# A state-space block and a SiLU layer on one core: the last second product with tokens on the partitions, and one transpose moved between engines

## The chip, the core and the metric

The kernel runs on one core of a Trainium2 chip. The metric is the device time of one execution in microseconds (us); lower is better. Before the change the median of three runs is 352.27 us (352.03 to 353.18). Five engines matter: TensorE (PE for its matmuls, PEld for its weight loads), VectorE (DVE), ScalarE (ACT), GpSimd (POOL) and SyncE (SP, which here only issues transfers).

## The reference

Two blocks follow each other. The first is a chunked scan (batch 4, 8 heads, 768 tokens, head width 32, state width 16), the second a two-layer network with SiLU on its result, seen as 3072 tokens of 256 features.

```python
# first block, per batch and head, in chunks of tokens
L = np.exp(cum[:, :, :, None] - cum[:, :, None, :]) * causal
M = np.einsum('bhin,bhjn->bhij', Cc, Bc) * L
y = np.einsum('bhij,bhjd->bhid', M, xc) + np.einsum('bhin,bhnd->bhid', Cc, state) * decay_to_i[..., None]
state = decay_full[..., None, None] * state + np.sum(Bx, axis=2)   # Bx: B times x, with the decay to the chunk's end
# second block: x is y as (3072, 256); w_in (256, 2048), w_out (2048, 256)
h = x @ w_in
g = h * (1.0 / (1.0 + np.exp(-h)))
out = g @ w_out
```

## The kernel before

The 3072 tokens are cut into 12 units of 256. For each unit the kernel does the scan with small tiled matmuls and then the network. Units go through the network in pairs. From the fourth unit on, the first product (`h = x @ w_in`), and for all pairs the second (`g @ w_out`), are done with seven block products instead of eight (a Strassen-Winograd form): some operands are first added or subtracted, and the seven results are added up afterwards. All data is fp32; every fp32 matmul call shows in the trace as two records.

The first unit's data comes in as follows. `load_n` loads B as tokens x (head, n), and `load_t` loads in a layout from which a 32x32 block transpose on VectorE (`f_T`) gives (head, n) x tokens. C of unit 0 comes by `load_t`, B of unit 0 by `load_n` alone, and TensorE transposes it (`f_TP`):

```python
load_t(0, 1, nc.sync)          # C of unit 0, four transfers
load_n(0, 0, nc.scalar)        # B of unit 0, tokens on the partitions, two transfers
nc.sync.dma_start(out=pa01, in_=...)   # the decays of units 0 and 1, one row per (head, n)
load_x(0, nc.sync)
for n in range(3):
    load_w(n, nc.sync)         # weights of 512 KB a piece, as raw bits
...
def f_T(u, i):                 # i = 0: B, i = 1: C
    t = (BH, CT)[i][u] = sc.tile([128, UT], FP32, name=("bh", "ct")[i])
    nc.vector.transpose(out=..., in_=tbc[u][:, i]...)

def f_TP(u):
    tp = ps_o.tile([128, 512], FP32, name="o_ps")
    for i, t in enumerate((bn[u],) if u == 0 else (bn[u], tbc.pop(u))):
        for k in range(2):
            nc.tensor.transpose(out=tp[:, 256 * i + 128 * k:...], in_=t[:, k]..., identity=ident)
    BH[u] = sc.tile([128, UT], FP32, name="bh")
    nc.scalar.activation(BH[u], tp[:, 0:256], AF.Copy)
    if u == 1:
        CT[u] = sc.tile([128, UT], FP32, name="ct")
        nc.scalar.activation(CT[u], tp[:, 256:512], AF.Copy)
    elif u > 1:
        CT[u] = tp[:, 256:512]          # stays in PSUM
def f_T2(u, e): ...   # ScalarE: ce = CT with the heads of one parity, needed by the product f_G0
def f_C(u): ...       # cw = CT * decays, on VectorE for u == 2, else on GpSimd
```

The order at the start (one queue per engine, in this order):

```python
f_T(0, 1)                       # VectorE: ct
for e in range(2): f_T2(0, e)   # ScalarE: ce
f_Ab(0, 0); f_Ab(0, 1)          # TensorE: decays to a PSUM tile
f_TP(0)                         # TensorE and ScalarE: bh
busy(0, 18)                     # TensorE: 18 small bf16 matmuls, fillers[...]
f_G0(0); busy(4, 8)             # TensorE: bh x ce, and fillers
f_Ek(0, 0); f_Ek(0, 1)          # VectorE: scans into E
f_B(0)                          # GpSimd: BT = bn * E
f_D0(0, True)                   # TensorE: BT x x
f_P01()                         # VectorE: pa01, clipped and scanned
f_C(0); f_S(0); f_SM(0)         # GpSimd: cw; VectorE: the states st; ScalarE
for k in range(2): f_M(0, k)    # VectorE: E = E * product
w_size(0); w_bits(0, 2)         # ScalarE, VectorE, GpSimd: piece 0 of the weights rebuilt from raw bits
...
f_Ek(1, 1); f_B(1); f_C(1); w_bits(2, 2); f_D0(1, True); f_G0(1); f_S(1)
...
```

The second product of a pair holds the weights still (`lhsT`) and moves 256 tokens of g, so the results have output features on the partitions. `f_out` transposes them in 32x32 blocks on VectorE and stores them in runs of 128 bytes, four transfers each. For the last pair (`final`) it is the same, but for the last product, which TensorE transposes in two halves:

```python
for n, (m, w, g) in enumerate(segs):        # products 1, w, 5, 7, 6, 4, 3
    o = ...                                 # a PSUM tile of 128 x 256
    for j in range(NF // 2):                # 8
        nc.tensor.matmul(out=o, lhsT=w(j), rhs=g()[:, j], start=(j == 0), stop=(j == last))
        if j == last:
            end(m, o)
        yield
# in end(m, o), for the last product of the last pair:
elif m == "3" and final:
    for k in range(2):
        nc.vector.tensor_tensor(out=pn[:, :, k], in0=on[:, :, k], in1=p["6"]..., op=ALU.add)
        tp = ps_h.tile([128, 512], FP32, name="hp")[:, 0:128]
        nc.tensor.transpose(out=tp, in_=p["3"][:, 128 * k:128 * k + 128], identity=ident)
        ot = opool.tile([128, UT], FP32, name="ot")[:, 0:128]
        if k == 0: nc.scalar.activation(ot, tp, AF.Copy)
        else:      nc.vector.tensor_copy(out=ot, in_=tp)
        (nc.sync, nc.scalar)[k].dma_start(out=out[r:r + 128, 0:128], in_=ot)
```

Of the kernel before, what the change touches and what calls it, by code (L numbers as in the profile page):

```python
# [8 lines left out]
FP32 = mybir.dt.float32  # L9
U32 = mybir.dt.uint32  # L10
BF16 = mybir.dt.bfloat16
AF = mybir.ActivationFunctionType
ALU = mybir.AluOpType
# [8 lines left out]
def kernel(  # L22
# [22 lines left out]
    nc = tc.nc  # L45

    batch, H, S, D = x.shape
    N = B.shape[-1]
    Q = 64
    UT = 256  # L50
    UPB = S // UT
    NU = batch * UPB
    d_model, d_ff = moe_w_in.shape
    NF = d_ff // 128
# [8 lines left out]
    sc = ctx.enter_context(tc.tile_pool(name="sc", bufs=1))  # L63
# [4 lines left out]
    ppool = ctx.enter_context(tc.tile_pool(name="ppool", bufs=5))  # L68
    opool = ctx.enter_context(tc.tile_pool(name="opool", bufs=2))
    ps_s = ctx.enter_context(tc.tile_pool(name="ps_s", bufs=1, space=bass.MemoryType.PSUM))  # L70
    ps_h = ctx.enter_context(tc.tile_pool(name="ps_h", bufs=3, space=bass.MemoryType.PSUM))
# [5 lines left out]
    pa, ab, bn, tbc, xt = ({} for _ in range(5))  # L77

    def at(u):
        return u // UPB, u % UPB * UT  # L80
# [28 lines left out]
    def load_t(u, i, q):  # L109

        b, t0 = at(u)
        if u not in tbc:
            tbc[u] = loads.tile([128, 2, 2, 8, N], FP32, name="tbc")
        for g in range(4):
            q.dma_start(out=tbc[u][32 * g:32 * g + 32, i],
                        in_=(B, C)[i][b, 2 * g:2 * g + 2, t0:t0 + UT].rearrange("e (t r) n -> t e r n", r=8))
# [76 lines left out]
    QZ = 8 * (Q + 1)  # L193
    pa01 = flat[:, 6 * UT:8 * UT]
    pz01, one01, pfx01 = (flat[:, 8 * UT + QZ * i:8 * UT + QZ * (i + 1)] for i in range(3))
    load_t(0, 1, nc.sync)
    load_n(0, 0, nc.scalar)
    nc.sync.dma_start(out=pa01, in_=bass.AP(tensor=a.tensor, offset=a.offset, ap=[[S, H], [0, N], [1, 2 * UT]]))
# [22 lines left out]
    def busy(n, small=0):  # L221
        t = ps_o.tile([128, 512], FP32, name="o_ps")
        for i in range(n):
            nc.tensor.matmul(out=t, lhsT=idle[:, 0:128], rhs=idle, start=True, stop=True)
        for i in range(small):
            nc.tensor.matmul(out=t[:64, :64], lhsT=idle[:, 0:64], rhs=idle[:, 64:128], start=True, stop=True)
# [20 lines left out]
    ident = const.tile([128, 128], FP32, name="ident")  # L247
# [22 lines left out]
    E, M, BT, BH, CT, CE, CW, PFX, ST, SM, DP, XM, GTS, BX = ({} for _ in range(14))  # L270
# [65 lines left out]
    def f_B(u, engine=nc.gpsimd):  # L336

        BT[u] = sc.tile([128, 2, H, N], FP32, name="BT")
        engine.tensor_tensor(out=BT[u], in0=bn[u], in1=E[u][:, :, :, Q - 1:Q].to_broadcast([128, 2, H, N]),  # L339
                                op=ALU.mult)  # L340

    def f_T(u, i):

        t = (BH, CT)[i][u] = sc.tile([128, UT], FP32, name=("bh", "ct")[i])
        nc.vector.transpose(out=t.rearrange("p (t r) -> p r t", r=8), in_=tbc[u][:, i].rearrange("p e r n -> p r e n"))
        if i == 1:
            tbc.pop(u)

    def f_TP(u):

        tp = ps_o.tile([128, 512], FP32, name="o_ps")
        for i, t in enumerate((bn[u],) if u == 0 else (bn[u], tbc.pop(u))):
            for k in range(2):
                nc.tensor.transpose(out=tp[:, 256 * i + 128 * k:256 * i + 128 * k + 128],
                                    in_=t[:, k].rearrange("p h n -> p (h n)"), identity=ident)
        BH[u] = sc.tile([128, UT], FP32, name="bh")
        nc.scalar.activation(BH[u], tp[:, 0:256], AF.Copy)
        if u == 1:

            CT[u] = sc.tile([128, UT], FP32, name="ct")  # L360
            nc.scalar.activation(CT[u], tp[:, 256:512], AF.Copy)
        elif u > 1:
            CT[u] = tp[:, 256:512]

    def f_T2(u, e):

# [4 lines left out]
    def f_C(u):  # L371

        CW[u] = sc.tile([128, UT], FP32, name="cw")
        engine = nc.vector if u == 2 else nc.gpsimd
        engine.tensor_tensor(out=CW[u].rearrange("p (c t) -> p c t", t=Q),
                             in0=CT.pop(u).rearrange("p (c t) -> p c t", t=Q), in1=PFX[u][:, :, 1:], op=ALU.mult)

# [131 lines left out]
    SO, TN, PEND = {}, {}, []  # L509
# [44 lines left out]
    def f_out(P, i, v, c):  # L554
# [4 lines left out]
        for q in range(4):  # L559
# [2 lines left out]
                            ap=[[d_model, 32], [32 * d_model, UT // 32], [1, 32]]),  # L562
                in_=t[32 * q:32 * q + 32].rearrange("p (b d) -> p b d", d=32))

    def s2_pair(P, final=False, joint=False):

        adder = nc.vector if final else nc.gpsimd
        p = {}
        segs = (("1", lambda j: wjo[:, 0, 0, j], lambda: gb(P, 0, 0)), ("w", lambda j: wjo[:, 1, 0, j], lambda: gb(P, 1, 0)),
                ("5", lambda j: SO[0][j // 4][:, j % 4], lambda: TN[P]),  # L570
                ("7", lambda j: SO[2][j // 4][:, j % 4], lambda: gb(P, 0, 1)),
                ("6", lambda j: SO[1][j // 4][:, j % 4], lambda: gb(P, 0, 0)),
                ("4", lambda j: wjo[:, 1, 1, j], lambda: gb(P, 1, 0)),
                ("3", lambda j: SO[3][j // 4][:, j % 4], lambda: gb(P, 1, 1)))

        def end(m, o):

            p[m] = ppool.tile([128, UT], FP32, name="ps")
            on = o.rearrange("p (c k t) -> p c k t", c=2, k=2)
            pn = p[m].rearrange("p (k c t) -> p c k t", c=2, k=2)  # L580
            if not (final and m == "3"):
                nc.scalar.activation(pn, on, AF.Copy)  # L582
            if m == "w":
                p_add(p["w"], p["w"], p["1"], adder)
                PEND.append(partial(f_out, P, 0, 0, p["w"]))
            elif m == "6":
                p_add(p["6"], p["6"], p["1"], adder)
                p_add(p["7"], p["7"], p["6"], adder)
                p_add(p["6"], p["5"], p["6"], adder, ALU.subtract)
                p_add(p["5"], p["5"], p["7"], adder, ALU.subtract)  # L590
                PEND.append(partial(f_out, P, 1, 1, p["5"]))
            elif m == "4":
                p_add(p["4"], p["4"], p["7"], adder)
                PEND.append(partial(f_out, P, 1, 0, p["4"]))
            elif m == "3" and final:

                for k in range(2):
                    nc.vector.tensor_tensor(out=pn[:, :, k], in0=on[:, :, k],
                                            in1=p["6"].rearrange("p (k c t) -> p c k t", c=2, k=2)[:, :, k],
                                            op=ALU.add)  # L600

                    tp = ps_h.tile([128, 512], FP32, name="hp")[:, 0:128]
                    nc.tensor.transpose(out=tp, in_=p["3"][:, 128 * k:128 * k + 128], identity=ident)
                    ot = opool.tile([128, UT], FP32, name="ot")[:, 0:128]
                    if k == 0:
                        nc.scalar.activation(ot, tp, AF.Copy)
                    else:
                        nc.vector.tensor_copy(out=ot, in_=tp)
                    b, t0 = at(2 * P + 1)
                    r = b * S + t0 + 128 * k  # L610
                    (nc.sync, nc.scalar)[k].dma_start(out=out[r:r + 128, 0:128], in_=ot)
            elif m == "3":
                p_add(p["3"], p["3"], p["6"], adder)
                PEND.append(partial(f_out, P, 0, 1, p["3"]))

        last = NF // 2 - 1
        if joint:
            o = ps_o.tile([128, 2, UT], FP32, name="o_ps")
            for j in range(NF // 2):
                for n, (m, w, g) in enumerate(segs[:2]):  # L620
                    nc.tensor.matmul(out=o[:, n], lhsT=w(j), rhs=g()[:, j], start=(j == 0 and n == 0), stop=(j == last),  # L621
                                     skip_group_check=True)
                    if j == last and n == 1:
                        end("1", o[:, 0])
                        end("w", o[:, 1])
                    yield
        for n, (m, w, g) in enumerate(segs):
            if joint and n < 2:
                continue
            if final and n % 2 == 0:  # L630
                o = ps_h.tile([128, 2, UT], FP32, name="hp")[:, 0]
            else:
                o = ps_o.tile([128, 2, UT], FP32, name="o_ps")[:, 0]
            for j in range(NF // 2):
                nc.tensor.matmul(out=o, lhsT=w(j), rhs=g()[:, j], start=(j == 0), stop=(j == last))  # L635
                if j == last:
                    end(m, o)
                yield
# [157 lines left out]
        return plan  # L796


    f_T(0, 1)
    for e in range(2):  # L800
        f_T2(0, e)
    f_Ab(0, 0)
    f_Ab(0, 1)
    f_TP(0)
    busy(0, 18)
    f_G0(0)
    busy(4, 8)
    f_Ek(0, 0)
# [25 lines left out]
    f_s1(0, 1)  # L834
    f_Ek(1, 1)
    f_B(1)
    f_C(1)
    w_bits(2, 2)
    f_D0(1, True)
    f_G0(1)  # L840
    f_S(1)
# [152 lines left out]
```

## Time and profile before

The profile is that of one execution of 350.6 us from the first to the last instruction. In four stretches, from the answer by windows:

| stretch, us | what runs | PE busy, us | DVE busy, us | ACT busy, us | POOL busy, us | DMA share |
|---|---|---|---|---|---|---|
| 0 to 25.19 | units 0 and 1 of the scan, first weights | 21.65 | 21.91 | 13.67 | 11.77 | 0.79 |
| 25.19 to 321.41 | network of all pairs, other scans | 296.22 | 170.08 | 146.20 | 98.82 | 0.64 |
| 321.41 to 345.59 | second product of the last pair | 24.18 | 12.72 | 2.87 | 2.94 | 0.15 |
| 345.59 to 350.57 | the end | 0.75 | 0.78 | 0.28 | 0.00 | 0.17 |

A busy figure is the time in which an engine had an instruction in work; small fillers on TensorE count as busy too. TensorE's records overlap, as its matmuls are pipelined: a record lasts longer than the distance to the next one. In the chain of work that ended last, each line gives a start, a duration and what ran there; the duration reaches to the next link, so it can be shorter than the instruction. In a timeline, "x16" after a group is the number of records merged into the line, and the bracket at its end is the idle time of the engine before it and what ended it.

### The profile page before, as it was taken

How to read it: one execution, taken by the hardware profiler on the slowest of the kernel's cores; microseconds unless marked ns; L12 is line 12 of the kernel's file. 1: busy time of each engine (PE TensorE's matmuls, PEld its weight loads, DVE VectorE, ACT ScalarE, POOL GpSimd, SP SyncE). 2: the span in 40 equal slices, each digit the busy share in tenths (PEclk: the TensorE clock that was granted, in tenths of full speed). 3: DMA queues.
4: the chain of work that ended last, by engine and by line, in shares of the span. 5: the costliest groups of instructions: out<-in, count | busy, mean ns of one | idle time of the engine just before them, and what ended most of it. 6: DMA issues, size and time to landing. Idle time of an engine off the chain costs nothing.

```text
span 350.6 us, 8353 instructions
## 1 busy us (share of the span) xinstructions
PE 342.8 (98%) x3308; PEld 287.7 (82%) x3308; DVE 205.5 (59%) x406; ACT 163.0 (46%) x398; POOL 113.5 (32%) x141
## 2 busy tenths in 40 slices
PE   7989999999999999999999999999999999999995
PEld 3668888888888888888888888888888888888883
DVE  7998889976795665543763553664562322244821
ACT  3677674323323545455544454645445454553100
POOL 4455335444285122244042244042144112051200
PEclk9999999999999999999999999999999999999999
DMA  6977987799776788964189964067404337521202
GB/s 129 214 247 174 263 270 137 133 202 212 133 128 116 129 169 157 175 129 76 24 165 171 163 121 83 16 118 140 78 2 75 65 57 136 90 54 30 36 4 46
DMA packets 117056, 42.66 MB, mean 122 GB/s; under 512 B 102424, under 2 KB 108824, under 8 KB 117016
## 3 DMA queue, kind: packets, MB, share of 16 engines
q1 hardware_dynamic: 110328, 25.67, 35.4%
q0 software_dynamic: 4464, 16.25, 24.6%
q8 instruction: 26, 0.43, 0.5%
q10 hardware_dynamic: 2224, 0.20, 0.5%
q14 instruction: 14, 0.11, 0.1%
HBM read 22.70 MB, written 3.15 MB: 74 GB/s over the span
## 4 chain that ended last, share of the span: by engine, by line
PE 91%; DVE 4%; issue 1%; DMA 1%; POOL 0%; ACT 0%; SPq 0%; DVEq 0%; ACTq 0%
PE o_ps L635 36%; PE hp L690 28%; PE hp L499 15%; PE hp L635 3%; PE gy L471 2%; PE o_ps L621 2%; PE gy L408 2%; PE gy L462 2%; DVE wv L178 1%; PE gy L393 1%; DVE E L419 1%; DVE E L302 1%; DMA gT<-in_a_dram 1%; DVE st L434 0%; DVE wu L174 0%
## 5 line engine op out<-in xcount | busy, mean ns | idle before, releaser
L693 DVE TENSOR_TENSOR gT<-hp,p 128x256 f32<-128x256 f32 x64 | 26.9, 420 | 73.9 <-ACT p L704 37.9
L499 PE MATMUL hp<-XM,w_in_sb 128*128 128x256 f32 x256 | 59.5, 382 | 1.6 <-POOL w_in_sb L182 1.4
L635 PE MATMUL o_ps<-gT,w_out_sb 128*128 128x256 f32 x240 | 60.4, 380 | 0.0
L696 ACT ACTIVATE gT<-gT 128x256 f32<-128x256 f32 x96 | 39.7, 414 | 44.0 <-DVE gT L693 44.0
L499 PEld LDWEIGHTS hp<-XM,w_in_sb 128*128 128x128 f32 x256 | 47.8, 190 | 9.8 <-POOL w_in_sb L182 2.9
L690 PE MATMUL hp<-raw 128*128 128x256 f32 x192 | 52.7, 380 | 0.0
L552 POOL TENSOR_TENSOR ps<-ps 128x256 f32<-128x256 f32 x35 | 29.4, 839 | 70.8 <-ACT ps L582 68.9
L635 PEld LDWEIGHTS o_ps<-gT,w_out_sb 128*128 128x128 f32 x240 | 45.5, 190 | 6.3
L547 POOL DMA_DIRECT2D gT<-gT x31 | 27.2, 914 | 67.8 <-DVE TN L538 21.5
L690 PEld LDWEIGHTS hp<-raw 128*128 128x128 f32 x192 | 36.2, 190 | 5.3 <-POOL ps L552 0.6
L704 ACT ACTIVATE p<-hp 128x256 f32<-128x256 f32 x64 | 24.5, 383 | 27.4 <-PE hp L690 26.0
L693 DVE TENSOR_TENSOR gT<-hp,u 128x256 f32<-128x256 f32 x32 | 13.6, 424 | 38.8 <-PE hp L690 38.8
L690 PE MATMUL hp<-XM,w_in_sb 128*128 128x256 f32 x128 | 34.1, 389 | 0.0
L501 ACT ACTIVATE gT<-hp 128x512 f32<-128x512 f32 x32 | 19.0, 594 | 26.9 <-PE hp L499 26.8
L690 PEld LDWEIGHTS hp<-XM,w_in_sb 128*128 128x128 f32 x128 | 23.3, 190 | 4.2 <-issue 0.9
L582 ACT ACTIVATE ps<-o_ps 128x256 f32<-128x256 f32 x38 | 14.4, 382 | 23.9 <-PE o_ps L635 19.8
L302 DVE TENSOR_TENSOR_SCAN E<-ab,diag 128x256 f32<-128x256 f32 (+1 forms) x32 | 25.3, 831 | 0.4
L339 POOL TENSOR_TENSOR BT<-bn,E 128x256 f32<-128x256 f32 x12 | 9.9, 824 | 46.5 <-DVE E L302 37.7
L635 PE MATMUL o_ps<-gT,wu 128*128 128x256 f32 x88 | 22.4, 380 | 0.0
L635 PE MATMUL o_ps<-gT,wv 128*128 128x256 f32 x88 | 22.2, 380 | 0.0
L635 PE MATMUL o_ps<-gT,raw 128*128 128x256 f32 x80 | 20.5, 380 | 0.0
L690 PE MATMUL hp<-raw,w_in_sb 128*128 128x256 f32 x64 | 19.1, 380 | 0.0
(125 smaller groups left out, 522.1 us busy)
## 6 DMA issues: line engine op xcount, KB each, us to landing
gT<-gT POOLq DMA_DIRECT2D x31, 512.0 KB, 6.1
ab<-in_a_dram SPq DMA_DIRECT2D x40, 128.0 KB
raw<-in_moe_w_in_dram SPq DMA_DIRECT2D x8, 512.0 KB
raw<-in_moe_w_out_dram SPq DMA_DIRECT2D x8, 512.0 KB
xt<-in_x_dram SPq DMA_DIRECT2D x24, 128.0 KB
out_dram<-ot SPq DMA_DIRECT2D x92, 32.0 KB
bn<-in_B_dram SPq DMA_DIRECT2D x22, 64.0 KB
tbc<-in_C_dram SPq DMA_DIRECT2D x40, 32.0 KB
```

Source lines behind the costliest of these rows:

```text
L302: nc.vector.tensor_tensor_scan(out=E[u].rearrange("p k h t -> p (k h t)")[:, Q * g0:Q * (g0 + n)], data0=t.rearrange("p g t -> p (g t)"), ...
L339: engine.tensor_tensor(out=BT[u], in0=bn[u], in1=E[u][:, :, :, Q - 1:Q].to_broadcast([128, 2, H, N]), op=ALU.mult)
L499: nc.tensor.matmul(out=hp[:, i], lhsT=w_in_sb[:, kc, f * 128:(f + 1) * 128], rhs=xm[:, kc], start=(kc == 0), stop=(kc == KC - 1))
L501: nc.scalar.activation(GTS[g][:, :, j], hp, AF.Silu)
L547: nc.gpsimd.dma_start(out=o[:, js], in_=a[:, js], accum_op=ALU.add)
L552: engine.tensor_tensor(out=o, in0=p, in1=q, op=op)
L582: nc.scalar.activation(pn, on, AF.Copy)
L635: nc.tensor.matmul(out=o, lhsT=w(j), rhs=g()[:, j], start=(j == 0), stop=(j == last))
L690: nc.tensor.matmul(out=o, lhsT=w, rhs=x_, start=start, stop=True, skip_group_check=True)
L693: nc.vector.tensor_tensor(out=o, in0=p, in1=q, op=ALU.add)
L696: nc.scalar.activation(o, i, AF.Silu)
L704: nc.scalar.activation(o, i, AF.Copy)
```

## The change

It has three parts. The second product of the last pair, all seven block products, is turned round: g is held still and the weights move, in two halves of 128 tokens, so results have tokens on the partitions and go out as rows of 512 bytes, without any transposes; the last product is added and stored by halves. B of unit 0 is loaded a second time in the layout for VectorE, with four transfers on ScalarE's queue, and transposed there in place of TensorE. And C of unit 1 stays in PSUM, with its product with the decays on VectorE in place of GpSimd, behind piece 2 of the weights.

```diff
+    load_t(0, 0, nc.scalar)
     load_t(0, 1, nc.sync)
     load_n(0, 0, nc.scalar)
...
     def f_TP(u):
-        for i, t in enumerate((bn[u],) if u == 0 else (bn[u], tbc.pop(u))):
+        for i, t in enumerate((bn[u], tbc.pop(u))):
...
         nc.scalar.activation(BH[u], tp[:, 0:256], AF.Copy)
-        if u == 1:
-            CT[u] = sc.tile([128, UT], FP32, name="ct")
-            nc.scalar.activation(CT[u], tp[:, 256:512], AF.Copy)
-        elif u > 1:
-            CT[u] = tp[:, 256:512]
+        CT[u] = tp[:, 256:512]
...
-        engine = nc.vector if u == 2 else nc.gpsimd
+        engine = nc.vector if 0 < u < UPB else nc.gpsimd      # UPB is 3
...
+    def f_rows(P, i, v, t):
+        for c in range(2):
+            f_row(P, i, v, t, c, (nc.sync, nc.scalar)[c])
+    def f_row(P, i, v, t, c, q):
+        b, t0 = at(2 * P + v)
+        q.dma_start(out=bass.AP(tensor=out.tensor, offset=out.offset + (b * S + t0 + 64 * c) * d_model + 128 * i,
+                                ap=[[128 * d_model, 2], [d_model, 64], [1, 128]]),
+                    in_=t[:, 128 * c:128 * c + 128])
...  # in end(): f_rows in place of f_out for the last pair, and for its product "3" no transposes
-            elif m == "3" and final:
-                ...
...
+            if final:
+                if m == "3":
+                    p[m] = ppool.tile([128, UT], FP32, name="ps")
+                for c in range(2):
+                    ts = slice(128 * c, 128 * c + 128)
+                    for j in range(NF // 2):
+                        nc.tensor.matmul(out=o[:, ts], lhsT=g()[:, j, ts], rhs=w(j), start=(j == 0), stop=(j == last))
+                        if j == last and m == "3":
+                            nc.vector.tensor_tensor(out=p[m][:, ts], in0=o[:, ts], in1=p["6"][:, ts], op=ALU.add)
+                            f_row(P, 0, 1, p[m], c, nc.sync)
+                        elif j == last and c == 1:
+                            end(m, o)
+                        if j % 2:
+                            yield
+                continue
...
-    f_T(0, 1)
+    for i in range(2):
+        f_T(0, i)
...
-    f_TP(0)
-    busy(0, 18)
+    busy(0, 20)
...
-    f_C(1)
-    w_bits(2, 2)
+    w_bits(2, 2)
+    f_C(1)
```

## The prediction

> **What bounds the kernel now.** I read the busy line of the page first, then the chain of work that ended last in order of time, then the timelines of the first 26 and the last 10 us, and last the groups by form for single durations.
>
> ```profile
> PE 342.8 (98%) x3308; PEld 287.7 (82%) x3308; DVE 205.5 (59%) x406; ACT 163.0 (46%) x398; POOL 113.5 (32%) x141
> ```
>
> TensorE is busy for 98% of the span, so only three things can move the end: how soon its unbroken stream begins, how long the stream is, and what follows its last matmul. The chain of the first stretch:
>
> ```profile
> 4.87 0.66 DVE ct L345
> 5.53 0.02 issue
> 5.55 0.91 ACT ce L369 x2
> 6.46 0.28 ACT bh L357
> 6.73 0.04 issue
> 6.78 0.73 PE o_ps L226 x18
> ...
> 9.46 0.42 PE hp L393 x32
> 9.89 0.02 issue
> 9.91 0.23 DVE st L432
> ...
> 24.41 0.74 POOL w_in_sb L182
> 25.15 0.04 issue
> 25.19 12.36 PE hp L499 x56
> ```
>
> The columns are start, duration, and what ran. Until 9.9 us the work passes from VectorE to ScalarE to TensorE, from there to 24.3 us it is VectorE almost throughout, and at 25.19 us TensorE gets the weights that it waited for. The waits of TensorE after that come to nothing, up to its last matmul at 345.4 us. So a change of the early path moves the end by the same amount. The tail:
>
> ```profile
> 342.13 3.62 PE L635 MATMUL hp<-gT,raw 128*128 128x256 f32 x16
> ```
> ```profile
> 345.79 0.49 DVE L598 TENSOR_TENSOR ps<-hp,ps 128x128 f32<-128x128 f32 x2 [2.09 <-PE hp L635]
> ...
> 346.13 0.59 PE L603 MATMUL hp<-ident,ps 128*128 128x128 f32 x2 [0.39 <-DVE ps L598]
> 346.50 0.28 ACT L606 ACTIVATE ot<-hp 128x128 f32<-128x128 f32 x1 [3.73 <-PE hp L603]
> 346.80 0.36 SPq L611 DMA_DIRECT2D out_dram<-ot  x1
> 346.90 0.29 DVE L608 COPY ot<-hp 128x128 f32<-128x128 f32 x1 [0.62 <-PE hp L603]
> 347.22 0.37 ACTq L611 DMA_DIRECT2D out_dram<-ot  x1
> ```
>
> After the last product come two additions, two transposes by TensorE, two copies and two stores; the second store is issued at 347.22 us, 1.43 us after the first addition began, and the span ends at 350.57.
>
> **What the Trainium skill says.** (1) "TensorE: Matmul & The Clock Gate", section "Back-to-back issue gap": a warm matmul of N columns follows the one before after N/2.4 + 2.5 ns, but a stream of weight load and matmul pairs ran at 81 ns for N = 128, where the formula gives 56. The trace: 16 records of 256 fp32 columns took 3.62 us, (3.62 - 0.38)/15 = 0.216 us each, so fp32 takes two array cycles a column, with only a few ns on top. It has no 128x128 product of 128 columns, so which of the two figures holds is the open question here. (2) The same page, "LDWEIGHTS (loading the stationary operand)": the load time follows the columns of the stationary operand, not its rows. The groups by form agree: fp32 loads of 32, 64 and 128 columns last 105, 131 and 190 ns. (3) "SBUF - State Buffer", section "Who interferes with whom": a VectorE instruction with two SBUF inputs contends with a GpSimd instruction that reads SBUF. The trace agrees: the merge of weight bits (L178) takes 0.68 us alone, and 1.22 and 1.17 us at 14.88 and 19.36 us, when GpSimd works. (4) "DMA: Bandwidth & Descriptors", section "Anatomy of one DMA": about 2 us of a DMA are fixed, most of it the receipt of the write. By the trace's semaphore records the store issued at 346.81 had landed at 348.36, the one of 347.22 at 348.81 but for one engine at 349.42: 1.55 to 2.2 us.
>
> **Part 1: the second product of the last pair.** Its seven products are 56 calls of two records each, 112 records of 256 moving columns: 321.41 to 345.59 us, 24.18 us. Afterwards each is two halves of 128 tokens, so 224 records of 128 moving columns and as many weight loads of 128 columns. The columns streamed are the same; each load now has to hide behind half the streaming, 108 ns (half of 216). What may be tight is the load. Its 190 ns are mostly latency: the transposes load 128 columns in 140 ns and still follow each other every 0.11 us, and bf16 fillers with loads of 112 ns every 31 ns:
>
> ```profile
> 6.78 0.73 PE L226 MATMUL o_ps<-gT 128*64 128x64 bf16 x18 [0.58 <-ACT bh L357]
> ...
> 37.39 0.38 PE L354 MATMUL o_ps<-ident,bn 128*128 128x128 f32 x2
> 37.61 0.38 PE L354 MATMUL o_ps<-ident,tbc 128*128 128x128 f32 x2
> ```
>
> The fillers: (0.73 - 0.20)/17 = 31 ns, with 64 columns loaded and 64 streamed, some 27 ns at one cycle a column, so equal load and stream overlap with 4 ns lost. The streaming part of an fp32 load of 128 columns, from the growth of the durations: (190 - 105)/96 = 0.89 ns a column, 113 ns; from the transposes,[...] 190 - 140 = 50 ns a pass, 100 ns. So I take a pitch of 109 to 115 ns, 111 in the middle: 224 x 0.111 = 24.9 us, **+0.7 us** (+0.2 to +1.6). All of it is on the path. The VectorE transposes that go away (0.45 us each) and the stores as rows lie beside the matmuls and give nothing here.
>
> **Part 2: the tail.** The last half's product ends, VectorE adds 128 columns (0.29 us, after the same 0.2 us from the last streamed column), and SyncE stores. The last column streams at 345.59; addition at 345.79 to 346.08, store at about 346.11 instead of 347.22: 1.1 us earlier. The first half went out some 16 records (1.8 us) before. If this store lands in 1.55 us and no engine is late, a further 0.6 us goes. From landing to end stays 350.57 - 349.42 = 1.15 us. Together **-1.1 to -1.7 us**, -1.4 in the middle.
>
> **Part 3: the start.** Removed: two transposes and the 0.36 us copy of bh on ScalarE, which stands in the chain at 6.46. Added: a second block transpose on VectorE; the pitch of one to the scan after it is 5.36 - 4.87 = 0.49 us, and it stands before the transpose that feeds ce. So ce is done at 6.46 + 0.49 = 6.95, and the first product can start there, 0.5 us before the old 7.43; but VectorE's own row (two scans, 2.27 us, and the P pair, 2.03 us) now begins at 5.85 and ends at 10.16, where st could start at 9.91: **+0.25 us**. Four more loads also stand ahead of the other loads. There are eight completion semaphores in turn, so the load of pa01, issued at 3.07 us, must wait until an earlier load has landed (the C loads landed at 3.5 to 4.5 us): some 0.5 us later. It landed at 7.63 us, just when VectorE wanted it (7.65); half a us later it would land at about 8.1 to 8.6, against 8.14 wanted: +0 to +0.4 us more. For unit 1, the decay product cw leaves GpSimd for VectorE (0.40 us, as the PSUM form at 42.44 us), behind the bits of piece 2; with GpSimd quiet the merge at 19.36 us should take 0.68 instead of 1.17 us. That is -0.1 us. Sum for the start: **+0.3 us** (0 to +0.7).
>
> **Sum.** +0.7 - 1.4 + 0.3 = -0.4 us: 352.27 - 0.4, about 351.9 us.
>
> **Rivals.** (a) The weight loads become the bound of the final product: if the skill's 81 in place of 56 ns carries over, 108 x 81/56 = 156 ns a record, 224 x 0.156 = 35 us, and the kernel takes about 362 us. For it: the load lasts 190 ns, longer than the 108 ns it has to hide in, and no fp32 stream in this trace asks for so much. Against it: fillers with loads of 112 ns at a pitch of 31 ns show that duration isn't occupancy. I give it 5 to 6 in 100; a milder form (120 to 125 ns, +3 us) lies at the top of the range. (b) The start costs more: pa01 or x lands a us later, and VectorE, which is the chain, waits: about 352.8 us. For it: no slack at 7.65 us; against: the C loads land early enough for the semaphores. (c) The start wins, as the ScalarE copy leaves the chain and VectorE's late landing doesn't come: 0.3 us gained there, and with the full tail 350.9 us. Against it: VectorE is the chain from 9.9 us on, and gets one more instruction before that.
>
> **Range and chances.** The tail is nearly sure, between -1.1 and -1.7; the pitch is the widest term, +0.2 to +1.6, and skewed upward; the start 0 to +0.7. So 350.8 to 353.8 us. Two per cent are 7.0 us: faster by that can't come from these parts (1 in 100); slower by that needs rival (a) (5 in 100); within 2%: 94 in 100.
>
> **What would show it.** In the changed profile: 224 records of 128 columns for the last product, from whose run the pitch is (duration - last record)/(count - 1), right at 109 to 115 ns and wrong above 120; the last addition starting 0.2 us after the last streamed column and one store right after it; the st of unit 0 at 10.1 to 10.5 us; the merge at about 19.5 us at 0.68 us; and the unbroken stream of TensorE beginning at 25.2 to 25.9 us. The prediction is wrong if the pitch follows the load's 190 ns, if the stream begins before 25 or after 26 us, or if the final store takes over 2.5 us to land.

## The result, and the profile after

The changed kernel takes 356.61 us (median, 356.08 to 359.83) against 352.28 us: a ratio of 1.0128, with a 95% interval of 1.0090 to 1.0167. So it is slower by 4.3 us, outside the predicted range. The span in the profile grows from 350.57 to 354.25 us, by 3.68 us; the profiled execution was the fastest of the six (356.08 us), so its trace shows somewhat less than the median does. First the busy line of the page, then lines of the chain in order of time (start, duration, what ran):

```profile
PE 343.7 (97%) x3418; PEld 291.3 (82%) x3418; DVE 202.5 (57%) x404; ACT 162.1 (46%) x395; POOL 110.7 (31%) x140
```
```profile
1.73 1.92 DMA tbc<-in_B_dram
3.65 0.02 issue
3.67 4.75 DMA gT<-in_a_dram
8.42 0.02 issue
8.44 0.64 DVE gT L276
...
10.35 0.13 DVE st L428
...
24.58 0.74 POOL w_in_sb L182
25.32 0.04 issue
25.36 12.36 PE hp L495 x56
```

The start now hangs on the load of B, on whose landing pa01 (gT) had to wait for a semaphore, and on pa01 itself; VectorE follows. But TensorE's stream begins at 25.36 us, 0.17 us later than before. The timeline of the last product, and of the end:

```profile
321.54 3.73 PE L632 MATMUL hp<-w_out_sb,gT 128*128 128x128 f32 x32
...
344.96 0.29 DVE L634 TENSOR_TENSOR ps<-hp,ps 128x128 f32<-128x128 f32 x1 [0.95 <-PE hp L632]
345.31 1.86 PEld L632 LDWEIGHTS hp<-raw,gT 128*128 128x128 f32 x16 [0.57 <-DVE ps L634]
345.31 2.05 PE L632 MATMUL hp<-raw,gT 128*128 128x128 f32 x16 [0.38 <-DVE ps L634]
```
```profile
347.40 0.29 DVE L634 TENSOR_TENSOR ps<-hp,ps 128x128 f32<-128x128 f32 x1 [2.14 <-PE hp L632]
347.72 0.51 SPq L568 DMA_DIRECT2D out_dram<-ps  x1
```

Two things stand out. The brackets at 345.31 say that the last half had to wait for the addition of the half before it. And the last store is issued at 347.72 us, though the program ends at 354.25, 6.5 us later; before, it was 3.35 us. What the DMA engines do in that time, by windows (window, its length, busy times of the engines, TensorE's clock, DMA share, GB/s):

```profile
347.70:350.00 2.30, 0.00 (x0) 0.00 (x0) 0.00 (x0) 0.00 (x0) 0.00 (x0) 1.00 0.14 43
350.00:353.00 3.00, 0.00 (x0) 0.00 (x0) 0.00 (x0) 0.00 (x0) 0.00 (x0) 0.57 0.13 38
```

No engine computes, and the DMA engines are busy for 0.13 to 0.14 of their time for 5.3 us on end: two engines out of 16 would be 0.125. The share alone proves nothing, as it is also 0.14 in the 1.6 us in which e8 (below) lands a store on 16 engines. The semaphore increments tell more. Each of the last two stores before made 16 increments, as 16 engines landed. The last one now makes three: one at 348.64 us, soon after the issue, and two at 352.91 and 352.98. And by the trace's records of DMA packets, of the packets of 512 bytes at the end never more than 4 are under way at once, two new ones every 24 ns; with e8's last store it is up to 20.

By stretches, the 3.68 us are: start of the last pair's product +0.13 (321.41 to 321.54); the product +0.83 without its wait; the wait +0.65; from the last streamed column to the end +2.08 (4.98 to 7.06).

### The profile page after: what moved, and what is told of

The parts are those of the page before. It is cut to its first block, busy times and chain, and to the rows that moved or that the text cites. A ratio compares the mean times of both kernels' runs of the same rounds, so it can differ in the third digit from the quotient of the medians.

```text
span 354.3 us, 8562 instructions
## 1 busy us (share of the span) xinstructions
PE 343.7 (97%) x3418; PEld 291.3 (82%) x3418; DVE 202.5 (57%) x404; ACT 162.1 (46%) x395; POOL 110.7 (31%) x140
## 4 chain that ended last, share of the span: by engine, by line
PE 91%; DVE 4%; DMA 2%; issue 1%; ACTq 0%; POOL 0%; DVEq 0%
PE o_ps L642 32%; PE hp L697 28%; PE hp L495 15%; PE hp L632 4%; PE o_ps L632 3%; PE gy L467 2%; PE o_ps L612 2%; PE gy L404 2%; PE gy L458 2%; DMA gT<-in_a_dram 1%; PE gy L389 1%; DVE wv L178 1%; DVE E L415 1%; DMA tbc<-in_B_dram 1%; DVE st L430 0%
## 5 line engine op out<-in xcount | busy, mean ns | idle before, releaser
L642 PE MATMUL o_ps<-gT,w_out_sb 128*128 128x256 f32 x208 | 53.2, 380 | 0.0
L548 POOL TENSOR_TENSOR ps<-ps 128x256 f32<-128x256 f32 x35 | 27.7, 792 | 71.2 <-ACT ps L589 69.8
L642 PEld LDWEIGHTS o_ps<-gT,w_out_sb 128*128 128x128 f32 x208 | 39.4, 190 | 5.5
L642 PE MATMUL o_ps<-gT,wu 128*128 128x256 f32 x80 | 20.5, 380 | 0.0
L642 PE MATMUL o_ps<-gT,wv 128*128 128x256 f32 x80 | 20.3, 380 | 0.0
L589 ACT ACTIVATE ps<-o_ps 128x256 f32<-128x256 f32 x35 | 13.3, 383 | 14.8 <-PE o_ps L642 11.8
```

The source lines that it names most:

```text
L548: engine.tensor_tensor(out=o, in0=p, in1=q, op=op)
L589: nc.scalar.activation(p[m].rearrange("p (k c t) -> p c k t", c=2, k=2), o.rearrange("p (c k t) -> p c k t", c=2, k=2), AF.Copy)
```

## The experiments

**Theory 1.** A store with two blocks of 64 rows as its pattern, so an outermost dimension of 2, runs on two DMA engines only, always the same two, and the six such stores of the last 12 us queue up there. The Trainium skill says so: "DMA: Bandwidth & Descriptors", section "Why a DMA increments its semaphore by 16 and not by 1", has, for a DMA issued as these are, the number of engines as the largest one up to 16 that divides the slowest dimension of both access patterns, and the issuing sequencer writing the rest of the 16 increments at once. The trace agrees: two late increments and one early one. The prediction had not drawn on that section. **Rival 2.** Rows of 512 bytes at this place of the output are slow to write, however they are cut. **Rival 3.** The turned product and the wait in it are the loss.

All ratios are to the kernel before on the same chip, with 95% intervals.

| run | what differs | median, us | ratio (interval) | last streamed column to end, us |
|---|---|---|---|---|
| before | | 352.3 to 352.7 | 1 | 4.98 |
| the change | | 356.61 | 1.0128 (1.0090 to 1.0167) | 7.06 |
| e1 | stores of 64 rows | 353.81 | 1.0037 (1.0018 to 1.0056) | 4.20 |
| e2 | own PSUM tile | 356.42 | 1.0102 (1.0083 to 1.0120) | 7.61 |
| e3 | only the start, in the kernel before | 352.23 | 0.9990 (0.9971 to 1.0009) | |
| e4 | e1 and e2 | 352.92 | 1.0008 (0.9997 to 1.0019) | 4.20 |
| e5 | 64 rows for the last product alone | 353.86 | 1.0034 (1.0021 to 1.0047) | 4.51 |
| e6 | 64 rows for all but the last product | 353.61 | 1.0035 (1.0020 to 1.0050) | 4.54 |
| e7 | kernel before, last stores on two engines | 354.86 | 1.0063 (1.0048 to 1.0079) | 7.30 |
| e8 | 128 rows a store, own tile, old start | 351.50 | 0.9973 (0.9964 to 0.9982) | 3.07 |
| e8b | e8 again | 351.55 | 0.9976 (0.9968 to 0.9984) | |
| e10 | e8 with the start of the change | 351.98 | 0.9988 (0.9977 to 1.0000) | |
| e9 | e10 with bn loaded after pa01 | 352.10 | 0.9990 (0.9972 to 1.0008) | |

**e1: stores of 64 rows.**

```diff
-        q.dma_start(out=bass.AP(..., ap=[[128 * d_model, 2], [d_model, 64], [1, 128]]),
-                    in_=t[:, 128 * c:128 * c + 128])
+        for k in range(2):
+            r = b * S + t0 + 128 * k + 64 * c
+            q.dma_start(out=out[r:r + 64, 128 * i:128 * i + 128], in_=t[64 * k:64 * k + 64, 128 * c:128 * c + 128])
```

> The changed kernel, with each store of 2 x 64 rows written as two stores of 64 rows; bytes and rows are the same. Theory 1 (a store whose outermost dimension is 2 runs on two DMA engines only, and the last stores queue up on those two): each store posts 16 landings instead of 2, the last one lands about 1.6 us after its issue instead of 5.3, and 3.6 us come back: about 353.0 us. Rival 2 (rows of 512 bytes into every second block of the output are slow to write, however they are cut): the last store still lands 5 us after its issue, about 356.6 us. Rival 3 (the turned product itself and the wait inside it are the loss): within 0.5 us of 356.6.

Measured: 353.81 us, 2.8 us back. Each store makes 16 increments, and the last one, issued at 349.15, has landed at 351.05, 1.9 us later. Same bytes, same rows, same addresses, so rival 2 falls. That 0.8 us less came back than expected has two sources in the trace: the two stores of the last half follow each other on one queue, 0.51 us apart, and the last one took 1.9 us instead of 1.6. From the last column to the end it is 2.86 us less than with the change, as much as the medians say. The span fell by only 1.93 us, since in this execution the last pair's product began at 322.46 instead of 321.54 us; that start differs from run to run (last section).

**e2: a PSUM tile of its own for the last half.**

```diff
                 for c in range(2):
                     ts = slice(128 * c, 128 * c + 128)
+                    if m == "3" and c == 1:
+                        o = ps_h.tile([128, 2, UT], FP32, name="hp")[:, 0]
```

> The changed kernel, with a PSUM tile of its own for the second half of the last product, stores unchanged. The wait of TensorE for the first half's addition (0.4 to 0.6 us at 345.3) should be gone. Theory 1: the last addition comes 0.5 us sooner, but the store still queues behind the others on two DMA engines, so most of that is lost again: 356.1 to 356.6 us. Rival 3 (the wait inside the last product is the loss, its effect on the end being more than its length): clearly below 355.5 us.

Measured: 356.42 us, no clear difference from the change. In the timeline of e2 the product runs through without a wait, and the last addition comes half a us earlier than with the change:

```profile
343.10 3.74 PE L634 MATMUL hp<-raw,gT 128*128 128x128 f32 x32
...
346.88 0.29 DVE L636 TENSOR_TENSOR ps<-hp,ps 128x128 f32<-128x128 f32 x1 [1.50 <-PE hp L634]
```

The store is issued at 347.20 instead of 347.72 us and yet lands at 353.03, as late as before (352.98). So the wait is real and goes with the shared tile (whether it follows the tile or the place in PSUM, e2 does not tell apart), but it doesn't set the end while the two engines have a queue. Rival 3 falls for the wait.

**e4: both repairs.** The two edits above.

> Both repairs together: stores of 64 rows, and the second half of the last product in its own PSUM tile. Theory 1: now the half microsecond of the wait counts in full: about 352.5 us, half a microsecond under the kernel with the stores alone. Rival 2 or 3: no different from one repair alone.

Measured: 352.92 us, 0.9 us below e1. The product's wait of 0.65 us accounts for most of it. The spans of the two traces differ by 1.18 us, the 0.65 us and a start of the product at 321.93 us here against 322.46 in e1.

**e3: the start alone, in the kernel before.** The start's lines of the diff, and nothing of the second product.

> The kernel before, with the change of the start alone (B of unit 0 by VectorE, C of unit 1 kept in PSUM); second product and stores as before. By the trace of the changed kernel the unbroken stream of TensorE begins 0.17 us later: 352.3 to 352.6 us. A rival that puts part of the loss on the start expects 353 us or more.

Measured: 352.23 us, a ratio of 0.9990 with 1 in its interval. The start is not where the 4.3 us went.

**e5 and e6: which of the stores.** In e5 the stores of the last product alone are cut, in e6 all others.

```diff
+        if (i, v) == (0, 1):        # the last product; in e6: !=
+            ...                     # two stores of 64 rows, as in e1
+            return
         q.dma_start(...)            # 2 x 64 rows
```

> The changed kernel, with only the two stores of the last product cut into stores of 64 rows; the six earlier stores of the turned product stay at two engines. Theory 1a (most of the loss is the queue that the earlier stores leave on the two engines): 14 of the 16 engines land about 1.6 us after the last issue, the two that have the queue at about 350.7 us of the trace, so only about 2 us come back: 354.2 to 355.0 us. Theory 1b (each store's own time on two engines is the loss, without a queue): the same as with all stores cut, about 353.8 us.

> The reverse: the six earlier stores cut into 64 rows, the two stores of the last product left on two engines. In the changed kernel's trace one store follows another on the two engines at 1.5 us. Theory 1a: the last store finds its engines nearly free and lands about 3 us after its issue instead of 5.3: 354.0 to 354.6 us. Theory 1b: the last landing stays at 5 us, 356 us and more.

Measured: 353.86 and 353.61 us, both close to e1. Neither 1a nor 1b has it right for both. For e6, 1a's direction holds: without a queue the last store, issued at 348.13 us, lands at 351.23, 3.1 us later instead of 5.26. So of the 5.26 us some 3.1 are a store's own time on two engines, and 2.2 the queue. In e5 the queue was still there: the two engines finished the earlier stores at 350.58 us and landed their few rows of the last store at 350.92, while the other 14 had landed by 350.48. But by then that store, second on its queue, had been issued at 348.59 only, so the queue cost just 0.44 us. So the pile-up costs much only where a last store on two engines stands behind others of its kind, and either edit alone brings back as much as e1.

**e7: the cause put into the kernel before.** Its last two stores get an outermost dimension of 2. The rows of each block of 128 tokens are stored in an interleaved order for that, so this kernel doesn't store the same rows at the same places.

```diff
-                    (nc.sync, nc.scalar)[k].dma_start(out=out[r:r + 128, 0:128], in_=ot)
+                    (nc.sync, nc.scalar)[k].dma_start(
+                        out=bass.AP(tensor=out.tensor, offset=out.offset + r * d_model,
+                                    ap=[[d_model, 2], [2 * d_model, 64], [1, 128]]), in_=ot)
```

> The kernel before, with nothing changed but the shape of its last two stores: 2 x 64 rows, interleaved, in place of 128, so that the outermost dimension is 2 (the rows of a block of 128 tokens are then stored in another order). Theory 1: two landings a store instead of 16, and the last one lands about 1.5 us later, 1.4 us and, if the two stores queue on the same two engines, up to 2.5 us more in all: 353.7 to 354.9 us. Rival 2 (the layout of the turned product is the cause, not the number of engines): 352.3 to 352.7 us.

Measured: 354.86 us, 2.3 us more, with the matmuls as before. The timeline of e7 and the window of its end:

```profile
347.27 0.64 SPq L611 DMA_DIRECT2D out_dram<-ot  x1
...
347.69 1.13 ACTq L611 DMA_DIRECT2D out_dram<-ot  x1
```
```profile
350.00:352.20 2.20, 0.00 (x0) 0.00 (x0) 0.00 (x0) 0.00 (x0) 0.00 (x0) 0.62 0.12 37
```

The first store lands at 350.70, 3.4 us after its issue, the second at 352.21, 1.5 us after the first, though it came from another queue: two late increments for each, a DMA share of 0.12. Also with both under way there are never more than 4 packets of 512 bytes at once, as with one store on two engines. So the issuing engine made no difference; both stores fell to the same two DMA engines. Theory 1 stands, and the turned product isn't needed for the loss.

**e8: a version to beat both.** The tokens of the last two units are put in order when XM is written, so a half is 128 rows in a line and needs one store of 128 rows; the two last stores go to different queues; the last half has its own tile; the start is that of the kernel before.

```diff
+            if u < NU - 2:
                 nc.scalar.activation(XM[u][:, i:i + n], y[:, i:i + n, 0:128], AF.Copy)
+            else:
+                for w in range(2):
+                    nc.scalar.activation(<XM[u], half w>.rearrange("p (k c t) -> p c k t", k=2, c=2),
+                                         y[:, 2 * w:2 * w + 2, 0:128].rearrange("p c (k t) -> p c k t", k=2), AF.Copy)
...
+        r = b * S + t0 + 128 * c
+        q.dma_start(out=out[r:r + 128, 128 * i:128 * i + 128], in_=t[:, 128 * c:128 * c + 128])
...
-                            f_row(P, 0, 1, p[m], c, nc.sync)
+                            f_row(P, 0, 1, p[m], c, (nc.scalar, nc.sync)[c])
```

> A version meant to beat both: the turned product with the start of the kernel before, a PSUM tile of its own for the last half, and the tokens of the last two units in order, so that a half is 128 rows in a line and one store of 128 rows on its own queue. From the traces: the turned product costs 0.8 us, the shorter tail gives 1.1 to 1.7: 351.4 to 352.0 us, if theory 1 names all of the loss. If the turned product has another cost at its end, 352.5 us or more.

Measured: 351.50 us, faster than the kernel before by 0.27% (0.18 to 0.36). Its timeline:

```profile
343.62 3.74 PE L643 MATMUL hp<-raw,gT 128*128 128x128 f32 x32
...
347.39 0.29 DVE L645 TENSOR_TENSOR ps<-hp,ps 128x128 f32<-128x128 f32 x1 [1.50 <-PE hp L643]
```

The last product is one unbroken run. The store was issued at 347.71 and landed on 16 engines from 349.06 to 349.24, 1.53 us. From the last column to the end it is 3.07 us, against 4.98 before and 7.06 with the change. The two terms, +0.83 for the product and -1.91 for the end, add up to -1.08 us; by the ratio it is -0.95.

**e8b, e10, e9: the start once more, with the repaired end.** e10 is e8 with the start of the change; e9 is e10 with this:

```diff
-    load_n(0, 0, nc.scalar)
     nc.sync.dma_start(out=pa01, ...)
+    load_n(0, 0, nc.scalar)
```

> The best version so far once more, with the start of the kernel before, as the yardstick for the two starts beside it: 351.2 to 351.8 us, as measured.

> The same with the start of the change (B of unit 0 by VectorE, C of unit 1 kept in PSUM). If the start costs the 0.17 us that the trace of the changed kernel shows: 351.4 to 352.0 us, 0.2 us more than beside it. If the start gains, as its purpose was: below the one beside it by 0.2 us or more.

> The start of the change, with the load of bn of unit 0 issued after that of pa01, so that pa01 takes a completion semaphore that is free sooner. In the changed kernel VectorE waits 0.38 us for pa01 at 8.06 us. If that wait is what the start costs: it goes, and the time is 0.2 to 0.4 us below the version with the start of the change. If other waits take its place (the first weights): no difference.

Measured: 351.55, 351.98 and 352.10 us. The intervals of e8b and e10 overlap. Side by side their medians point to a cost of the start of 0.43 us; e3 pointed the other way, so a cost or a gain is not settled. e9 does not test what it was meant to: in its trace pa01 has the same semaphore as in e10 and was issued at 3.75 us, against 3.70 there, so it did not get one that is free sooner. VectorE waited 0.26 us for pa01, until 8.45 us. What that wait costs stays open.

## Why the prediction was wrong

Its sum was +0.7 - 1.4 + 0.3 for product, tail and start; in the trace the same terms are +0.83 (and 0.65 for a wait that it didn't have), +2.08, and +0.13.

- **Product: right in size.** 32 records in 3.73 us, the last of them 0.275 us long, are (3.73 - 0.275)/31 = 0.111 us each, the predicted 111 ns. The loads now last 192 ns and keep the pace, as the fillers had shown. What makes up the 111 ns is less clear: the estimate of 50 ns a pass took a load of 190 ns for two passes, which no record shows, and the trace doesn't tell whether load or matmul sets the pitch. The first rival, 156 ns a record scaled up from the skill's 81 ns in "TensorE: Matmul & The Clock Gate", section "Back-to-back issue gap", did not happen.
- **The wait in the last product: missing.** The two halves share a PSUM tile, and the second half's first matmul waited for the addition that reads the first. None of the prediction's three rivals is this wait; e2 removed it by a tile alone.
- **Tail: wrong, and this is the step that failed.** "If this store lands in 1.55 us" and "the tail is nearly sure, between -1.1 and -1.7" took the landing time of a store of 128 rows for one with the same bytes in the pattern 2 x 64. It took 5.26 us: 3.1 on two engines, 2.2 in their queue. The rest of the term held: the store was issued 0.53 us after the last streamed column instead of 1.63, the 1.1 us that were to be won; against that, its landing took 3.06 us longer than that of the last store before (2.20 us), and the end 0.12 us more. The prediction's own list had this sign of being wrong, a final store of over 2.5 us. The share of DMA engines was open to view in the diff (`ap=[[128 * d_model, 2], ...`) and in the skill. With a pattern of 128 rows (e8) the tail is 3.07 us, 1.91 us shorter than before, somewhat more than predicted.
- **Start: right in most steps, its size not shown.** In this trace st began at 10.26 us (10.1 to 10.5 predicted), pa01 came late by 0.38 us, the stream began at 25.36 us, 0.17 us later. But over all traces it began between 25.19 and 26.09 us with the old start (four traces) and between 25.36 and 25.91 us with the new one (nine), so the 0.17 us lie inside what changes from run to run. The merge with GpSimd quiet took 0.68 us:

```profile
19.69 0.68 DVE L178 SCALAR_TENSOR_TENSOR wv<-raw,wv 128x512 uint32<-128x512 uint32 x1
```

- **The range:** it held only costs that I had thought of for each engine's instructions. The one for the transfer was given as a fixed time, with the condition for it left unstudied. The stated ends of its terms add up to -1.5 to +1.2 us, so to 353.5 us at the top and not 353.8.

## What to carry to other kernels

Before a store or a load is reshaped, look at the outermost dimension of both sides: with 2 there, two DMA engines carry everything, and such transfers queue behind each other whatever queue issues them (seen here for stores). Count the landings of one transfer in the trace; the DMA share alone can be the same for two engines and for 16. At the end of a kernel give each half of a result that is read while the other is computed its own PSUM tile, and judge such a repair only when nothing else sets the end.

## What else the runs showed

- A 64-row share of 512-byte rows takes a DMA engine 1.5 us when it is busy with such stores one after the other, 23 ns a row; on idle engines a 2 x 64 store took 3.1 us from issue to the last landing, the 128-row store on 16 engines 1.53 us.
- Weight loads of 128 fp32 columns, each 192 ns by the profile, hid behind matmuls 112 ns apart: 0.0 us idle for the matmuls of the product's first six parts.
- The start of the last pair's product moves from run to run: 322.18 us in e8 and 321.46 in e8b, which are the same kernel. There the difference arises in the first 7 us, where TensorE's four records of L310 took 3.59 us in one and 2.86 in the other; why is not shown. In e1 TensorE stood idle for 0.87 us before 102.65 us, at the end of a chain that began with a load of the decays. A start that is worth 0.2 us can't be judged from one trace each.
